# Folding a linear-attention weight by head groups instead of by 128-row blocks

## The chip, the cores and the metric

The kernel runs on one core of one Trainium2 chip. The metric is the device time of one execution in microseconds (us). With one core there is one span and one granted clock of the tensor engine per execution. PE is the tensor engine (PEld its weight loads), DVE the vector engine, ACT the scalar engine, POOL GpSimd, SP the sync engine, whose queue issues most DMA transfers. In the profiles `psT` is PSUM, the memory that PE writes, and `reg` and most other names are SBUF; an *eviction* is a copy from PSUM to SBUF by ACT or DVE.

## The reference

```
xn  = layernorm(x)                              # x: 2048 x 640
# A: linear attention, 32 heads of 20
q, k, v = split(xn @ wqkv)                      # each 32 heads x 2048 x 20
pq, pk  = phi(q), phi(k)                        # phi(t) = (t>0 ? t+1 : exp(t)) + 1e-6
kv  = einsum("bhsd,bhse->bhde", pk, v)          # 20 x 20 for each head
den = einsum("bhqd,bhd->bhq", pq, sum_s pk) + 1e-6
s   = concat_heads((pq @ kv) / den) @ wo        # 2048 x 640
# B: gate
g   = silu(relu(xn @ w1) @ w2)                  # w1: 640 x 1728
out = x + s * g
```

The arrays are bfloat16.

## The kernel before

The kernel never forms v. It builds G = xn' pk (640 x 640, "Gram blocks", line 790), then the key-value product as wv' G with everything outside a head's own 20 x 20 block masked to zero (line 805), and multiplies that by wo. The result is a *folded weight* `wf` (640 x 640), in five blocks of 128 rows. An output tile is then one product, pq (already divided by its denominator) times `wf` (line 891), multiplied by the gate and added to x.

A head has 20 rows, so 128 rows hold 6.4 heads. The masked product is made in six chunks of six heads (120 columns; the last has two heads, 40 columns). A block of 128 rows of `wf` always needs two of these chunks, and what the mask doesn't write has to be zero. That is why there is a memset and why each block sums two products:

```python
VR = 6 * DH      # 120
VC = 6           # chunks
# ... cut ...
    def kv_block(c, b):
        # ... cut: n0, n1, nh, r0, m0 of chunk c; five matmuls into ps[b] ...
        sc.op("DVE", lambda eng: eng.tensor_tensor(
            out=kvp[:, c, n0:n1].rearrange("p (h e) -> p h e", e=DH),
            in0=ps[b][:, 0:n1 - n0].rearrange("p (h e) -> p h e", e=DH),
            in1=mv6[:, m0:m0 + nh].unsqueeze(2).to_broadcast([P, nh, DH]), op=ALU.mult),
            R=[("ps", b), ("mv6", m0), ("kvz",)], W=[("kv", c)])

    def W_block(m, b):
        cs = [c for c in range(VC) if VR * c < P * (m + 1) and min(VR * (c + 1), D) > P * m]
        fns = []
        for a in range(2):
            for ci, c in enumerate(cs):
                fns.append(lambda eng, a=a, c=c, ci=ci: eng.matmul(
                    ps[b + a][:, 0:HN], lhsT=kvp[:, c, P * m:P * (m + 1)], rhs=wo_sb[:, c, HN * a:HN * (a + 1)],
                    start=(ci == 0), stop=(ci == len(cs) - 1)))
        # ... cut: the group, then ACT (even m) or DVE (odd m) copies ps to wf[:, m, :] ...

    sc.op("POOL", lambda eng: eng.memset(kvp, 0.0), W=[("kvz",)], extra=[lastG])
    # ... cut ...
    hooks = {
        (0, 0): [kvs],                                    # key-value chunks, division of pq
        (1, 0): [lambda: W_block(0, 0), lambda: W_block(1, 2)],
        (1, 1): [lambda: W_block(2, 0), lambda: W_block(3, 2)],
        (1, 2): [lambda: W_block(4, 0)],
        (2, 0): [s_of(0, 0, 4)],                          # first output tile
        # ... cut ...
    }
```

`sc` is a small scheduler: `R` and `W` are what an operation reads and writes, and it puts in the semaphore waits. A hook `(p, i)` runs after the i-th group of 13 gate matmuls of tile pair p; the folded weight and the output tiles are thus woven between the gate matmuls, and PE goes through all of it in program order.

Of the kernel before, what the change touches and what calls it, by code (L numbers as in the profile page):

```python
# [5 lines left out]
ACTF = mybir.ActivationFunctionType  # L6
# [14 lines left out]
class Sched:  # L21
# [69 lines left out]

    def _hazards(self, R, W):
        agents = []
        for key in R:
            st = self.res.get(key)
            if st is not None and st.w is not None:
                agents.append(st.w)
        for key in W:
            st = self.res.get(key)
            if st is not None:  # L100
                if st.w is not None:
                    agents.append(st.w)
                agents.extend(st.r.values())
        return agents

    def _update_res(self, agent, R, W):
        Rset = set(R)
        for key in R:
            st = self.res.get(key)
            if st is None:  # L110
                st = self.res[key] = _Res()
            rk = agent if agent[0] == "D" else agent[0]
            st.r[rk] = agent
            st.nread += 1
        for key in W:
            st = self.res.get(key)
            if st is None:
                st = self.res[key] = _Res()
            else:
                assert (st.w is None or st.nread > 0 or key in Rset or key in self.allow_unread  # L120
                        or (agent[0] == "PE" and st.w[0] == "PE")), (
                    "unread overwrite of %r by %r (prev writer %r)" % (key, agent, st.w))
            st.w = agent
            st.r = {}
            st.nread = 0

    def op(self, E, fn, R=(), W=(), extra=()):
        return self.group(E, [fn], R, W, extra)

# [85 lines left out]
def bass_recurrent_scan__linear_attn_block__dense_activation_relu__prompt_kernel(  # L215
# [9 lines left out]
    Bb, S, D = A_x.shape  # L225
# [4 lines left out]
    P = 128  # L230
    T = S // P
    J = S // 512
    C = D // P
# [3 lines left out]
    HN = D // 2  # L237
    EPS_LN = 1e-5
    XR = 8
    VR = 6 * DH  # L240
    VC = 6
# [16 lines left out]
    reg3 = nc.alloc_sbuf_tensor("reg3", [P, T * D], bf)  # L258
    pk = reg3[:, :].rearrange("p (t n) -> p t n", t=T)
    kvp = reg3[:, 0:VC * D].rearrange("p (c n) -> p c n", c=VC)  # L260
# [3 lines left out]
    pqT = nc.alloc_sbuf_tensor("pqT", [P, C, S], bf)  # L264
# [12 lines left out]
    wf = reg6[:, C * D:2 * C * D].rearrange("p (c n) -> p c n", c=C)  # L277
# [4 lines left out]
    wo_sb = reg7[:, 0:VC * D].rearrange("p (c n) -> p c n", c=VC)  # L282
# [17 lines left out]
    mv6 = nc.alloc_sbuf_tensor("mv6", [P, 8], f32)  # L300
# [13 lines left out]
    ps = [psT[:, 512 * i:512 * (i + 1)] for i in range(8)]  # L314

    def ps2(b, n):
        return psT[:, 512 * b:512 * (b + 2)].rearrange("p (a n) -> p a n", a=2)[:, :, 0:n]
# [4 lines left out]
    sc = Sched(nc, NDS)  # L322
    nds = [0]

    def dma(E, fn, R=(), W=(), extra=()):
        i = nds[0]
        nds[0] += 1
        return sc.dma(E, fn, i, R=R, W=W, extra=extra)

    def tok(t):  # L330
        return slice(P * t, P * (t + 1))
# [34 lines left out]
    for k in range(KA, C):  # L366
# [15 lines left out]
          R=[("ident",)], W=[("ident",)])  # L382
# [341 lines left out]
    for j in range(J):  # L724
        for n, item in enumerate(plans[j]):
# [33 lines left out]
            if j == J - 1 and n == 0:  # L759
                for c in range(VC):  # L760
                    r0 = VR * c if c < VC - 1 else D - P
                    dma("SP", lambda eng, c=c, r0=r0: eng.dma_start(wo_sb[:, c, :], A_wo[r0:r0 + P, :]),
                        W=[("wo", c)], extra=[last_norm[0]])
# [12 lines left out]
    for a in range(2):  # L776
# [3 lines left out]
            W=[("w2", a)], extra=[lastW1])  # L780
    for u in range(2):
        dma("ACT", lambda eng, u=u: eng.dma_start(w2l[64 * u:64 * (u + 1), :], B_w2[NF * P:FF, :]),
            W=[("w2l", u)], extra=[lastW1])


    def G_block(k, b):
        fns = []
        for t in range(T):
            for a in range(2):
                fns.append(lambda eng, t=t, a=a: eng.matmul(  # L790
                    ps[b + a][:, 0:HN], lhsT=xn[:, t, P * k:P * (k + 1)], rhs=pk[:, t, HN * a:HN * (a + 1)],
                    start=(t == 0), stop=(t == T - 1)))
        ag = sc.group("PE", fns, R=[("xn", t) for t in range(T)] + [("pk", t) for t in range(T)],
                      W=[("ps", b), ("ps", b + 1)])
        sc.op("DVE", lambda eng: eng.tensor_copy(GT[:, k, :].rearrange("p (a n) -> p a n", a=2), ps2(b, HN)),  # L795
              R=[("ps", b), ("ps", b + 1)], W=[("GT", k)])
        return ag

    def kv_block(c, b):
        n0 = VR * c  # L800
        n1 = min(n0 + VR, D)
        nh = (n1 - n0) // DH
        r0 = VR * c if c < VC - 1 else D - P
        m0 = 0 if c < VC - 1 else 6
        sc.group("PE", [(lambda eng, k=k: eng.matmul(ps[b][:, 0:n1 - n0], lhsT=wv_sb[:, k, r0:r0 + P],  # L805
                                                     rhs=GT[:, k, n0:n1], start=(k == 0), stop=(k == C - 1)))
                        for k in range(C)], R=[("wv",)] + [("GT", k) for k in range(C)], W=[("ps", b)])
        sc.op("DVE", lambda eng: eng.tensor_tensor(
            out=kvp[:, c, n0:n1].rearrange("p (h e) -> p h e", e=DH),
            in0=ps[b][:, 0:n1 - n0].rearrange("p (h e) -> p h e", e=DH),  # L810
            in1=mv6[:, m0:m0 + nh].unsqueeze(2).to_broadcast([P, nh, DH]), op=ALU.mult),
            R=[("ps", b), ("mv6", m0), ("kvz",)], W=[("kv", c)])

    def W_block(m, b):
        cs = [c for c in range(VC) if VR * c < P * (m + 1) and min(VR * (c + 1), D) > P * m]
        fns = []
        for a in range(2):
            for ci, c in enumerate(cs):
                fns.append(lambda eng, a=a, c=c, ci=ci: eng.matmul(  # L819
                    ps[b + a][:, 0:HN], lhsT=kvp[:, c, P * m:P * (m + 1)], rhs=wo_sb[:, c, HN * a:HN * (a + 1)],  # L820
                    start=(ci == 0), stop=(ci == len(cs) - 1)))
        sc.group("PE", fns, R=[("wo", c) for c in cs] + [("kvz",)] + [("kv", c) for c in cs],
                 W=[("ps", b), ("ps", b + 1)])
        if m % 2 == 0:
            sc.op("ACT", lambda eng: eng.activation(out=wf[:, m, :].rearrange("p (a n) -> p a n", a=2), in_=ps2(b, HN),
                                                    func=ACTF.Copy), R=[("ps", b), ("ps", b + 1)], W=[("wf", m)])
        else:
            sc.op("DVE", lambda eng: eng.tensor_copy(wf[:, m, :].rearrange("p (a n) -> p a n", a=2), ps2(b, HN)),
                  R=[("ps", b), ("ps", b + 1)], W=[("wf", m)])



# [56 lines left out]
    def s_mm(t, lo, hi, b):  # L889
        i = t // 4  # L890
        sc.group("PE", [(lambda eng, c=c: eng.matmul(  # L891
            ps[b][:, 0:hi - lo], lhsT=pqT[:, c, tok(t)], rhs=wf[:, c, lo:hi],
            start=(c == 0), stop=(c == C - 1))) for c in range(C)],
            R=[("pqT", i, c) for c in range(C)] + [("wf", c) for c in range(C)], W=[("ps", b)])

    def s_tile(t, b):
        os_ = so[0] % NOUT
        so[0] += 1
        for a in range(2):
            s_mm(t, HN * a, HN * (a + 1), b + a)  # L900
        s_out(t, os_, 0, 0, D, ps2(b, HN), [("ps", b), ("ps", b + 1)], 2)

    def s_last(t):
        for i in range(3):
            lo, hi = LC[i], LC[i + 1]
            s_mm(t, lo, hi, LB[i])
            s_out(t, NOUT, i, lo, hi, ps[LB[i]][:, 0:hi - lo].unsqueeze(1), [("ps", LB[i])], 1)

    lastG = None
    for k in range(C):  # L910
        lastG = G_block(k, (0, 2, 0, 2, 4)[k])
    sc.op("POOL", lambda eng: eng.memset(kvp, 0.0), W=[("kvz",)], extra=[lastG])
    for jx in range(4):
        dma("SP", lambda eng, jx=jx: eng.dma_start(
            xre[:, 4 * jx:4 * jx + 4, :], x2[512 * jx:512 * (jx + 1), :].rearrange("(t p) n -> p t n", p=P)),
            W=[("xre", jx)], extra=[lastG])

    def s_of(p, u, b):
        return lambda: s_tile(pairs[p][u], b)

    def kvs():
        for c in range(VC):
            kv_block(c, (6, 7, 4, 5, 2, 3)[c])
        for i in (0, 1, 2, 3):
            divide(i)

    hooks = {
        (0, 0): [kvs],
        (1, 0): [lambda: W_block(0, 0), lambda: W_block(1, 2)],
        (1, 1): [lambda: W_block(2, 0), lambda: W_block(3, 2)],  # L930
        (1, 2): [lambda: W_block(4, 0)],
        (2, 0): [s_of(0, 0, 4)],
        (2, 1): [s_of(0, 1, 6)],
        (2, 2): [s_of(1, 0, 4)],
# [60 lines left out]
```

## Time and profile before

| | before |
|---|---|
| time, median of four runs | 223.42 us (223.0 to 223.94) |
| span of the profiled execution | 221.3 us |
| PE busy | 215.9 us, 98% |
| granted clock | 1.00 |
| first gate matmul to first output matmul (below: *the stage*) | 20.80 us |

The page's first part (busy time, share of the span, instructions):

```profile
PE 215.9 (98%) x1437; PEld 134.2 (61%) x1447; DVE 119.2 (54%) x221; ACT 82.9 (37%) x136; POOL 46.9 (21%) x69
```

What PE's matmuls waited for (total us, times, longest), the whole answer of the wait view for PE:

```profile
PE psT L388 <- DVE zero L378: 1.1, 1, 1.1
PE psT L571 <- issue: 0.2, 1, 0.2
```

The chain that ended last, in order of time, through the stage (start, length, engine and line, number of instructions). L842 are gate matmuls, L805 the key-value chunks, L819 the folded weight, L860 the gate's last 64 rows, L891 output tiles:

```profile
132.32 1.77 PE psT L842 x13
134.09 1.43 PE psT L805 x30
135.52 5.30 PE psT L842 x39
140.82 0.65 PE psT L860 x8
141.47 1.87 PE psT L842 x13
143.34 1.09 PE psT L819 x8
144.43 1.77 PE psT L842 x13
146.20 1.09 PE psT L819 x8
147.28 1.77 PE psT L842 x13
149.05 0.54 PE psT L819 x4
149.59 3.53 PE psT L842 x26
153.12 1.36 PE psT L891 x10
```

Every piece is PE and each starts where the one before ends. So in this stage time is the number of matmuls times their spacing: 5.30 us for 39 is 136 ns each; such a place in PE's stream is called a *slot* below. The folded weight takes 1.09 + 1.09 + 0.54 = 2.72 us for 20 matmuls, 136 ns each too. Note the 1.87 us after the eight L860 matmuls, where 13 matmuls usually take 1.77: there the weights go from 64 rows back to 128.

Two groups off the chain matter for the argument (the groups view; the last column is idle time of that engine before them, and what ended it):

```profile
L912 POOL MEMSET reg<- 128x3840 bf16 x1 | 3.3, 3298 | 36.2 <-PE psT L790 36.2
L808 DVE TENSOR_TENSOR reg<-psT,mv 128x120 bf16<-128x120 f32 (+1 forms) x6 | 1.1, 259 | 2.6 <-POOL reg L912 2.6
```

The memset takes 3.3 us, and DVE stands idle 2.6 us for it before the first masked eviction. That is a real wait, of an engine that nothing on the chain is waiting for.

### The profile page before, as it was taken

Reading aid. Unit: us, or ns where it says so; the run is one execution under the profiler, and the core shown is the slowest. Engines: PE = TensorE matmul, PEld = TensorE weight load, DVE = VectorE, ACT = ScalarE, POOL = GpSimd, SP = SyncE. Lnnn points to the kernel's source line nnn. Section 1 sums busy time; section 2 is a strip of 40 time slices with the busy share of each in tenths; the row PEclk is TensorE's granted clock in tenths of the full one; section 3 lists DMA queues with packets and bytes.
Section 4 is the critical chain, followed back from the end, with each engine's and each line's share of the span. In section 5 each row is a group of like instructions: output and inputs, shape, how many; then the busy total and the mean of one; then the engine's idle time right before and its main releaser. Section 6 shows DMA issues by size and latency. Waiting matters only on the chain.

```text
span 221.3 us, 3515 instructions
## 1 busy us (share of the span) xinstructions
PE 215.9 (98%) x1437; PEld 134.2 (61%) x1447; DVE 119.2 (54%) x221; ACT 82.9 (37%) x136; POOL 46.9 (21%) x69
## 2 busy tenths in 40 slices
PE   8999999999999999999999999999999999999993
PEld 7655554555545555444477777677767776776672
DVE  3798967789649999773511125920424240422243
ACT  4596575666655766554512000232021102110211
POOL 2268601220042699930000005000000000000000
PEclk9999999999999999999999999999999999999999
DMA  5988597611002152000199889800100100101012
GB/s 179 291 315 157 129 292 80 181 30 30 3 1 59 30 143 67 0 0 3 44 188 365 293 274 379 294 6 3 59 30 33 59 30 33 44 16 62 0 59 61
DMA packets 27904, 23.91 MB, mean 108 GB/s; under 512 B 12272, under 2 KB 27248, under 8 KB 27888
## 3 DMA queue, kind: packets, MB, share of 16 engines
q1 hardware_dynamic: 24656, 19.50, 31.5%
q10 hardware_dynamic: 3232, 4.18, 5.3%
q8 instruction: 11, 0.18, 0.3%
q14 instruction: 5, 0.04, 0.1%
HBM read 15.81 MB, written 5.24 MB: 95 GB/s over the span
## 4 chain that ended last, share of the span: by engine, by line
PE 93%; DMA 2%; SPq 2%; DVE 1%; issue 1%; ACT 0%; ACTq 0%; DVEq 0%
PE psT L842 26%; PE psT L571 25%; PE psT L790 10%; PE psT L549 10%; PE psT L891 9%; PE psT L496 8%; DMA reg<-in_A_x_dram 2%; PE psT L819 1%; PE psT L860 1%; PE psT L588 1%; SPq L359 1%; PE psT L805 1%; SPq L340 1%; PE psT L677 1%; DVE reg L881 0%
## 5 line engine op out<-in xcount | busy, mean ns | idle before, releaser
L842 PE MATMUL psT<-reg,hT 128*128 128x320 bf16 x416 | 60.5, 299 | 0.0
L842 PEld LDWEIGHTS psT<-reg,hT 128*128 128x128 bf16 x416 | 40.3, 98 | 16.5 <-issue 1.1
L571 PE MATMUL psT<-reg 128*128 128x512 bf16 x192 | 45.5, 379 | 0.3 <-issue 0.2
L881 DVE TENSOR_TENSOR reg<-psT,reg 128x640 bf16<-128x640 f32 (+2 forms) x18 | 13.5, 750 | 48.8 <-PE psT L891 47.6
L575 ACT ACTIVATE hT<-psT 128x512 bf16<-128x512 f32 x52 | 30.9, 600 | 18.7 <-PE psT L571 18.7
L571 PEld LDWEIGHTS psT<-reg 128*128 128x128 bf16 x195 | 18.9, 98 | 22.0 <-issue 0.4
L870 ACT ACTIVATE reg<-psT 128x640 bf16<-128x640 f32 x12 | 8.2, 702 | 43.1 <-PE psT L842 23.6
L891 PE MATMUL psT<-reg,pqT 128*128 128x320 bf16 (+2 forms) x165 | 24.4, 295 | 0.0
L507 POOL TENSOR_TENSOR zacc<-zacc,reg 128x640 f32<-128x640 f32 x16 | 23.8, 1488 | 2.3 <-DVE reg L531 1.3
L549 PE MATMUL psT<-reg 128*128 128x512 bf16 x95 | 23.8, 379 | 0.3
L790 PE MATMUL psT<-reg 128*128 128x320 bf16 x160 | 21.9, 299 | 0.0
L891 PEld LDWEIGHTS psT<-reg,pqT 128*128 128x128 bf16 x165 | 16.1, 98 | 5.8
L790 PEld LDWEIGHTS psT<-reg 128*128 128x128 bf16 x160 | 15.7, 98 | 6.2
L513 ACT ACTIVATE regE<-psT 128x640 bf16<-128x640 f32 x24 | 15.6, 701 | 9.1 <-PE psT L496 9.1
L496 PE MATMUL psT<-reg 128*128 128x320 bf16 x120 | 18.3, 299 | 0.0
L557 DVE TENSOR_SCALAR regE<-psT 128x512 bf16<-128x512 f32 x20 | 13.6, 682 | 8.2 <-ACT regE L556 8.2
L559 DVE SCALAR_TENSOR_TENSOR pqT<-regE 128x512 bf16<-128x512 bf16 x20 | 17.4, 869 | 0.7
L870 ACT ACTIVATE reg<-psT,rsy 128x640 bf16<-128x640 f32 x4 | 3.2, 794 | 38.6 <-PE psT L860 33.4
L549 PEld LDWEIGHTS psT<-reg 128*128 128x128 bf16 x100 | 9.8, 98 | 11.5
L496 PEld LDWEIGHTS psT<-reg 128*128 128x128 bf16 x120 | 11.7, 98 | 6.5 <-DMA reg<-reg 0.4
L795 DVE CAST reg<-psT 128x640 bf16<-128x640 f32 x5 | 4.1, 824 | 20.9 <-PE psT L790 20.9
L556 ACT ACTIVATE regE<-psT 128x512 bf16<-128x512 f32 x20 | 12.0, 598 | 8.5 <-PE psT L549 8.5
(68 smaller groups left out, 177.8 us busy)
## 6 DMA issues: line engine op xcount, KB each, us to landing
reg<-in_A_x_dram SPq DMA_DIRECT2D x16, 160.0 KB, 3.1
scr<-regE SPq DMA_DIRECT2D x4, 640.0 KB, 11.1
reg<-in_A_x_dram SPq DMA_DIRECT2D x4, 640.0 KB, 9.3
out_dram<-reg SPq DMA_DIRECT2D x15, 160.0 KB, 1.8
regE<-scr SPq DMA_DIRECT2D x4, 512.0 KB, 5.3
reg<-in_B_w_dram ACTq DMA_DIRECT2D x1, 1120.0 KB, 12.1
reg<-in_B_w_dram ACTq DMA_DIRECT2D x1, 1040.0 KB, 9.1
reg<-in_A_wo_dram SPq DMA_DIRECT2D x6, 160.0 KB, 3.7
```

What stands on the lines that cost most here:

```text
L496: fns.append(lambda eng, a=a, k=k, lhs=lhs: eng.matmul(ps[b + a][:, 0:HN], lhsT=lhs[:, k, tok(t)], rhs=wqk[:, k, D + HN * a:D + HN * (a + 1)],
L507: sc.op("POOL", lambda eng: eng.tensor_tensor(out=zacc[:, :], in0=zacc[:, :], in1=pk[:, t, :], op=ALU.add), R=[("zacc",), ("pk", t)], W=[( ...
L513: sc.op("ACT", lambda eng: eng.activation(out=o_.rearrange("p (a n) -> p a n", a=2), in_=ps2(b, HN), func=func, scale=scale), R=[("ps", b) ...
L549: sc.group("PE", [(lambda eng, k=k: eng.matmul(ps[b], lhsT=wqk[:, k, P * f:P * (f + 1)], rhs=xnT[:, k, schunk(j)], start=(k == 0), stop=(k ...
L557: sc.op("DVE", lambda eng: eng.tensor_scalar(out=r_, in0=ps[b], scalar1=0.0, scalar2=1e-6, op0=ALU.max, op1=ALU.add), R=[("ps", b), ("er_e ...
L559: sc.op("DVE", lambda eng: eng.scalar_tensor_tensor(out=pqT[:, f, schunk(j)], in0=e_, scalar=1.0, in1=r_, op0=ALU.min, op1=ALU.add), R=[(" ...
L571: a = sc.group("PE", [(lambda eng, k=k: eng.matmul(ps[b], lhsT=w1_sb[:, k, P * f:P * (f + 1)], rhs=src[:, k, :], start=(k == 0), stop=(k = ...
L575: sc.op("ACT", lambda eng: eng.activation(out=hT[:, f, schunk(j)], in_=ps[b], func=ACTF.Relu), R=[("ps", b)], W=[("hT", j, f)])
L790: fns.append(lambda eng, t=t, a=a: eng.matmul(ps[b + a][:, 0:HN], lhsT=xn[:, t, P * k:P * (k + 1)], rhs=pk[:, t, HN * a:HN * (a + 1)], sta ...
L842: sc.group("PE", [(lambda eng, f=f: eng.matmul(ps[b][:, 0:HN], lhsT=hT[:, f, tok(t)], rhs=w2_sb[:, f, HN * n:HN * (n + 1)], start=(f == 0 ...
L881: sc.op("DVE", lambda eng: eng.tensor_tensor(out=tmpo[:, os_, lo:hi].rearrange(shp, a=na), in0=src, in1=g_sb[:, t, lo:hi].rearrange(shp, a ...
L891: sc.group("PE", [(lambda eng, c=c: eng.matmul(ps[b][:, 0:hi - lo], lhsT=pqT[:, c, tok(t)], rhs=wf[:, c, lo:hi], start=(c == 0), stop=(c = ...
```

## The change

A chunk's masked product is non-zero only in its own 120 rows and columns. The change makes one pass for each chunk: 120 columns of weights, two matmuls (640 output columns in two halves), no accumulation, 12 matmuls instead of 20. Only columns that the mask has written are read, so the zero fill goes. The price: a pass yields rows 120c to 120c+119 of the folded weight at partitions 0 to 119, while the output matmuls want blocks of 128 rows. Ten SBUF to SBUF transfers move them, cut where a pass crosses a block boundary. The passes are also moved one place earlier.

```diff
--- before.py
+++ after.py
@@ -809,24 +809,32 @@
             out=kvp[:, c, n0:n1].rearrange("p (h e) -> p h e", e=DH),
             in0=ps[b][:, 0:n1 - n0].rearrange("p (h e) -> p h e", e=DH),
             in1=mv6[:, m0:m0 + nh].unsqueeze(2).to_broadcast([P, nh, DH]), op=ALU.mult),
-            R=[("ps", b), ("mv6", m0), ("kvz",)], W=[("kv", c)])
-
-    def W_block(m, b):
-        cs = [c for c in range(VC) if VR * c < P * (m + 1) and min(VR * (c + 1), D) > P * m]
-        fns = []
-        for a in range(2):
-            for ci, c in enumerate(cs):
-                fns.append(lambda eng, a=a, c=c, ci=ci: eng.matmul(
-                    ps[b + a][:, 0:HN], lhsT=kvp[:, c, P * m:P * (m + 1)], rhs=wo_sb[:, c, HN * a:HN * (a + 1)],
-                    start=(ci == 0), stop=(ci == len(cs) - 1)))
-        sc.group("PE", fns, R=[("wo", c) for c in cs] + [("kvz",)] + [("kv", c) for c in cs],
-                 W=[("ps", b), ("ps", b + 1)])
-        if m % 2 == 0:
-            sc.op("ACT", lambda eng: eng.activation(out=wf[:, m, :].rearrange("p (a n) -> p a n", a=2), in_=ps2(b, HN),
-                                                    func=ACTF.Copy), R=[("ps", b), ("ps", b + 1)], W=[("wf", m)])
+            R=[("ps", b), ("mv6", m0)], W=[("kv", c)], extra=[lastG])
+
+    wtmp = reg3[:, VC * D:2 * VC * D].rearrange("p (c n) -> p c n", c=VC)
+    wkeys = []
+
+    def W_block(c, b):
+        n0 = VR * c
+        n = min(VR, D - n0)
+        sc.group("PE", [(lambda eng, a=a: eng.matmul(
+            ps[b + a][0:n, 0:HN], lhsT=kvp[:, c, n0:n0 + n], rhs=wo_sb[:, c, HN * a:HN * (a + 1)],
+            start=True, stop=True)) for a in range(2)], R=[("wo", c), ("kv", c)], W=[("ps", b), ("ps", b + 1)])
+        dst = wtmp[0:n, c, :].rearrange("p (a n) -> p a n", a=2)
+        if c % 2 == 0 or c == 1:
+            sc.op("ACT", lambda eng: eng.activation(out=dst, in_=ps2(b, HN)[0:n], func=ACTF.Copy),
+                  R=[("ps", b), ("ps", b + 1)], W=[("wtmp", c)])
         else:
-            sc.op("DVE", lambda eng: eng.tensor_copy(wf[:, m, :].rearrange("p (a n) -> p a n", a=2), ps2(b, HN)),
-                  R=[("ps", b), ("ps", b + 1)], W=[("wf", m)])
+            sc.op("DVE", lambda eng: eng.tensor_copy(dst, ps2(b, HN)[0:n]), R=[("ps", b), ("ps", b + 1)],
+                  W=[("wtmp", c)])
+        q = n0
+        while q < n0 + n:
+            e = min(n0 + n, (q // P + 1) * P)
+            key = ("wf", q)
+            wkeys.append(key)
+            dma("SP", lambda eng, q=q, e=e: eng.dma_start(wf[q % P:q % P + e - q, q // P, :],
+                                                          wtmp[q - n0:e - n0, c, :]), R=[("wtmp", c)], W=[key])
+            q = e
 
 
 
@@ -891,7 +899,7 @@
         sc.group("PE", [(lambda eng, c=c: eng.matmul(
             ps[b][:, 0:hi - lo], lhsT=pqT[:, c, tok(t)], rhs=wf[:, c, lo:hi],
             start=(c == 0), stop=(c == C - 1))) for c in range(C)],
-            R=[("pqT", i, c) for c in range(C)] + [("wf", c) for c in range(C)], W=[("ps", b)])
+            R=[("pqT", i, c) for c in range(C)] + wkeys, W=[("ps", b)])
 
     def s_tile(t, b):
         os_ = so[0] % NOUT
...
-    sc.op("POOL", lambda eng: eng.memset(kvp, 0.0), W=[("kvz",)], extra=[lastG])
     for jx in range(4):
         dma("SP", lambda eng, jx=jx: eng.dma_start(
             xre[:, 4 * jx:4 * jx + 4, :], x2[512 * jx:512 * (jx + 1), :].rearrange("(t p) n -> p t n", p=P)),
@@ -926,9 +933,9 @@
 
     hooks = {
         (0, 0): [kvs],
-        (1, 0): [lambda: W_block(0, 0), lambda: W_block(1, 2)],
-        (1, 1): [lambda: W_block(2, 0), lambda: W_block(3, 2)],
-        (1, 2): [lambda: W_block(4, 0)],
+        (0, 1): [lambda: W_block(0, 4), lambda: W_block(1, 6)],
+        (1, 0): [lambda: W_block(2, 0), lambda: W_block(3, 2)],
+        (1, 1): [lambda: W_block(4, 0), lambda: W_block(5, 2)],
         (2, 0): [s_of(0, 0, 4)],
         (2, 1): [s_of(0, 1, 6)],
         (2, 2): [s_of(1, 0, 4)],
```

## The prediction

> **What bounds the kernel.** The tensor engine (PE). The page's first part gives PE 215.9 us busy of a 221.3 us span (98%); the chain that ended last is 93% PE; the wait view for PE holds 1.3 us in all; the granted clock is 1.00. From 132 to 153 us, where the change acts, the timeline shows no PE gap. So only PE instruction slots count, and any new PE wait.
>
> **What is removed.** The folded-weight matmuls. Before, five groups of 8, 8 and 4 (20 in all, 128x320): the chain in order of time gives 1.09, 1.09 and 0.54 us, together 2.72 us, 136 ns each. (The Trainium skill, "TensorE: Matmul & The Clock Gate", section "Back-to-back issue gap", gives N/2.4 + 2.5 ns, 136 ns for 320 columns; the trace agrees.) After, six passes of two matmuls, 12 in all, none accumulating: an estimated 12 x 136 = 1.63 us. Saved: 8 x 136 = 1.09 us, all on the chain. Fewer output rows (120, 40) do not make a matmul shorter: the 320 moving columns set it. Changing the weights' shape costs a little: after the 64-row group, 13 gate matmuls take 1.87 us instead of 1.77; the one 40-row pass may cost 0.1 us likewise.
>
> **The memset** (POOL, 3.30 us at 132.4) holds DVE's first masked eviction for 2.6 us, but PE doesn't wait for that: the 39 matmuls after it run at 136 ns. Its removal gives DVE slack, no time.
>
> **What is added.** Six evictions instead of five (ACT 0.70, DVE 0.82 us each, idle engines); the Silu table load (1.28 us) now follows the first two evictions on ACT, ending near 141. Ten SBUF to SBUF transfers on the SP queue, about 0.8 MB. Each occupies the queue about 0.43 us (160 KB loads in the SP timeline).
>
> **The new wait.** The first output matmul now waits for ten transfers. Estimated order: passes 0,1 at 137.3, passes 2,3 at 143.9, passes 4,5 at 146.2 to 146.7; evicted by about 147.7; the last three transfers issued by 149; landing 1.8 us later (160 KB output writes; the Trainium skill, "DMA: Bandwidth & Descriptors", "Anatomy of one DMA", has about 2.0 us fixed for the software-issued path), so near 151. PE has 39 gate matmuls (5.3 us) after the last pass, so it asks at about 152.0. About 1 us of slack: it should just hold. Ten semaphore waits before one matmul should be hidden by PE's queue: the five waits of a query block near 85 us left no gap in the chain.
>
> **Prediction.** 223.67 - 1.09 + 0.1 = 222.7 us (0.4% less). Range 222.0 to 223.7. Chances: faster by over 2% 0.01, within 2% 0.97, slower by over 2% 0.02.
>
> **What would show it.** Right: PE 8 matmuls fewer, folded-weight pieces of the chain about 1.6 us in place of 2.72; the first output matmuls start near 151.9 instead of 152.96, with no DMA in PE's waits; everything later shifts by the same 1 us; SP shows ten transfers landing by about 151. Wrong: PE waiting at the first output matmul for a transfer between its own buffers, or an issue gap there of some tenths.
>
> **What would make it wrong.** SBUF to SBUF transfers landing in 3 us or more, or a queue occupied longer than 0.43 us per issue: each us beyond the slack costs one us of PE. Second, the ten waits costing 0.3 us or more. Third, weights of 120 columns loading so slowly that they aren't hidden under 136 ns matmuls (up to 0.1 us per pass).

## The result, and the profile after

The changed kernel took 222.6 us (median of four runs, 222.55 to 222.66), against 223.42 us. The ratio is 0.9962 with a 95% interval of 0.9938 to 0.9986. All ratios here are the mean time of one kernel's fast runs over that of the other kernel's in the same rounds, so not quite the ratio of the medians.

The page's first part:

```profile
PE 214.9 (97%) x1429; PEld 133.6 (61%) x1439; DVE 119.7 (54%) x221; ACT 83.5 (38%) x137; POOL 43.5 (20%) x68
```

The whole wait view for PE has no transfer in it (L471 and L388 are at the kernel's start):

```profile
PE psT L388 <- DVE zero L378: 1.0, 1, 1.0
PE psT L471 <- DVE reg L462: 0.7, 1, 0.7
PE psT L571 <- issue: 0.2, 1, 0.2
```

The chain in order of time, through the same stage (L850 gate, L805 chunks, L820 folded weight, L868 the gate's last 64 rows, L899 output):

```profile
132.86 1.77 PE psT L850 x13
134.63 1.43 PE psT L805 x30
136.06 1.77 PE psT L850 x13
137.83 0.54 PE psT L820 x4
138.38 3.53 PE psT L850 x26
141.91 0.65 PE psT L868 x8
142.56 1.87 PE psT L850 x13
144.43 0.54 PE psT L820 x4
144.97 1.77 PE psT L850 x13
146.74 0.65 PE psT L820 x4
147.39 5.40 PE psT L850 x39
152.79 1.36 PE psT L899 x10
```

The stage went from 153.12 - 132.32 = 20.80 us to 152.79 - 132.86 = 19.93 us: 0.87 us less. Eight matmuls fewer are worth 8 x 136 ns = 1.09 us. The missing 0.21 us stands in two lines: the last piece of L820 takes 0.65 us where its sisters take 0.54, and the 39 gate matmuls after it take 5.40 us where before they took 5.30. That pass's second half is the one with 40 columns.

The spans differ by only 0.5 us, not 0.87, for two reasons. First, the stage began 0.54 us later in this execution. The chain says why: the first load of x, on which the first layernorm waits, took 4.96 us on the chain here and 4.40 us in the profile before. This differs between executions of one kernel too (the stage begins at 132.70 us here and at 131.81 in the profile of `after_again`), and is why the stage is the better measure below. Second, the tail, from the first output matmul to the end of the span, took 68.16 us here and 68.35 before, 0.19 us less; so 0.54 - 0.87 - 0.19 = -0.52. The difference lies in the last output writes and is no chance of these two profiles: the tail is 68.15 to 68.17 us in every profile with the ten transfers (except `late_two`, which has a slow clock there) and 68.35 to 68.59 in the three without them (`before`, `no_transfers`, `before_twelve`). Its cause was not looked into and stays open.

The lines that answer to the memset and the masked evictions (groups view):

```profile
L808 DVE TENSOR_TENSOR reg<-psT,mv 128x120 bf16<-128x120 f32 (+1 forms) x6 | 1.4, 268 | 1.2 <-PE psT L805 1.2
```

DVE's evictions now wait 1.2 us for their own matmuls and no longer for POOL. The ten transfers on SP's queue (timeline: start, length, the issues merged in one line):

```profile
138.87 11.73 SPq L835 DMA_DIRECT2D reg<-reg  x10
```

The last issue thus ends at 150.60 us. One single issue takes 0.52 to 0.98 us. The DMA view gives the time from issue to landing for some of the ten: 7.5 and 6.1 us for two of the first three, issued while the loads of x still kept the DMA engines busy (mean share 0.98 from 130 to 139 us and 1.06 from 139 to 144), and 1.8 to 2.2 us for those issued later. That the loads are the reason was not tested; the early ones had time to spare. The first output matmul starts at 152.63 us by the timeline.

### The profile page after: what moved, and what is told of

It reads as the page before. It is cut to its first block, busy times and chain, and to the rows that moved or that the text cites. A ratio compares the mean times of both kernels' runs of the same rounds, so it can differ in the third digit from the quotient of the medians.

```text
span 220.8 us, 3513 instructions
## 1 busy us (share of the span) xinstructions
PE 214.9 (97%) x1429; PEld 133.6 (61%) x1439; DVE 119.7 (54%) x221; ACT 83.5 (38%) x137; POOL 43.5 (20%) x68
## 4 chain that ended last, share of the span: by engine, by line
PE 92%; DMA 2%; SPq 2%; DVE 1%; issue 1%; ACT 0%; ACTq 0%; DVEq 0%
PE psT L850 26%; PE psT L571 25%; PE psT L790 10%; PE psT L549 10%; PE psT L899 9%; PE psT L496 8%; DMA reg<-in_A_x_dram 2%; PE psT L868 1%; PE psT L588 1%; SPq L359 1%; PE psT L820 1%; PE psT L805 1%; SPq L340 1%; PE psT L677 1%; DVE reg L889 0%
## 5 line engine op out<-in xcount | busy, mean ns | idle before, releaser
L850 PE MATMUL psT<-reg,hT 128*128 128x320 bf16 x416 | 60.5, 299 | 0.0
L850 PEld LDWEIGHTS psT<-reg,hT 128*128 128x128 bf16 x416 | 40.2, 98 | 16.6 <-issue 1.3
L899 PE MATMUL psT<-reg,pqT 128*128 128x320 bf16 (+2 forms) x165 | 24.4, 295 | 0.0
L899 PEld LDWEIGHTS psT<-reg,pqT 128*128 128x128 bf16 x165 | 16.1, 98 | 5.8
L417 DVE BATCH_NORM_STATS2 stats<-reg 128x6 f32<-128x320 bf16 x32 | 14.0, 474 | 2.0 <-DMA reg<-in_A_x_dram 2.0
```

Of the source, the lines that this page charges most:

```text
L417: sc.op("DVE", lambda eng: eng.bn_stats(stats[:, t, a, :], xv[:, HN * a:HN * (a + 1)]), R=[("xin", t % XR)], W=[("stats", t, a)])
L850: sc.group("PE", [(lambda eng, f=f: eng.matmul(ps[b][:, 0:HN], lhsT=hT[:, f, tok(t)], rhs=w2_sb[:, f, HN * n:HN * (n + 1)], start=(f == 0 ...
L899: sc.group("PE", [(lambda eng, c=c: eng.matmul(ps[b][:, 0:hi - lo], lhsT=pqT[:, c, tok(t)], rhs=wf[:, c, lo:hi], start=(c == 0), stop=(c = ...
```

## The experiments

The stage is measured from the start of the first gate matmul to the start of the first output matmul, in each profile. The kernel before ran in the same rounds. The experiments came in three batches, each on one chip.

| kernel | stage, us | time, us (median) | ratio to before [95%] | result |
|---|---|---|---|---|
| before | 20.80 | 223.42 | | |
| after | 19.93 | 222.60 | 0.9962 [0.9938, 0.9986] | correct |
| memset_back | 19.93 | 221.93 | 0.9957 [0.9931, 0.9984] | correct |
| eight_back | 21.02 | 223.46 | 1.0011 [0.9985, 1.0037] | correct |
| no_transfers | 19.93 | 222.61 | 0.9979 [0.9953, 1.0004] | wrong |
| pad128 | 19.72 | 222.39 | 0.9960 [0.9933, 0.9987] | correct |
| before_twelve | 19.72 | 222.07 | 0.9940 [0.9913, 0.9967] | wrong |
| narrow_two | 20.14 | 222.73 (one run) | | wrong |
| late_one | 20.48 | 223.05 | 0.9981 [0.9947, 1.0015] | correct |
| late_two | 22.56 | 226.34 | 1.0113 [1.0045, 1.0181] | correct |
| late_two_split | 21.92 | 224.28 | 1.0050 [1.0030, 1.0070] | correct |
| after_again | 19.93 | 222.00 | 0.9962 [0.9938, 0.9986] | correct |
| pad128_again | 19.72 | 221.80 | 0.9943 [0.9923, 0.9963] | correct |

The theory: only PE's instruction slots count in this stage, so the gain is the eight matmuls, less 0.2 us for the change of weight shape at the 40-column pass; everything else is hidden behind PE's work. The rivals: the memset's removal helps; the ten transfers, or the ten semaphore waits before the first output matmul, take some of the gain; the 0.2 us is something else.

### The memset back in

```diff
-            R=[("ps", b), ("mv6", m0)], W=[("kv", c)], extra=[lastG])
+            R=[("ps", b), ("mv6", m0), ("kvz",)], W=[("kv", c)], extra=[lastG])
...
+    sc.op("POOL", lambda eng: eng.memset(kvp, 0.0), W=[("kvz",)], extra=[lastG])
```

> The changed kernel with the memset of the key-value matrix back in its old place, and the masked evictions waiting for it. Theory (only PE slots count): same as the changed kernel, ratio to the kernel before about 0.996, 19.9 us from the first gate matmul after the Gram blocks to the first output matmul, as in the changed kernel (20.8 before), although the evictions start 1 us later. Rival (the memset's removal gives part of the gain): this stage grows towards 20.8 us.

The wait is back, by the groups view:

```profile
L808 DVE TENSOR_TENSOR reg<-psT,mv 128x120 bf16<-128x120 f32 (+1 forms) x6 | 1.1, 261 | 2.6 <-POOL reg L920 2.6
```

The stage is 19.93 us, as without it. A 3.3 us memset and a 2.6 us wait of DVE cost nothing here, to 0.01 us.

### Eight matmuls back

```diff
-            start=True, stop=True)) for a in range(2)], ...
+            start=True, stop=True)) for _ in range(2 if c < 4 else 1) for a in range(2)], ...
```

> The changed kernel with passes 0 to 3 issuing their two matmuls twice, so 20 matmuls again, same result. Theory: eight slots of 136 ns return, the stage is 19.93 + 1.09 = 21.0 us, time about 0.1% over the kernel before (ratio 1.000 to 1.002). Rival (the gain comes from something other than the number of matmuls): stays near 0.996.

The stage is 21.02 us, 1.09 more than the changed kernel's; each of the first two pairs of passes takes 1.09 us in the chain instead of 0.54. The time returns to that of the kernel before (1.0011).

### The transfers left out

```diff
-        q = n0
-        while q < n0 + n:
-            ...  # the transfers of this pass, key added for each
+        wkeys.append(("wtmp", c))
```

> Wrong result on purpose: the ten SBUF to SBUF transfers are left out, the output matmuls wait for the six evictions only and read stale weights. Theory (the transfers are hidden behind 39 gate matmuls): the stage stays 19.9 us, ratio 0.996. Rival (ten waits or late transfers cost part of the gain): 0.1 us or more shorter.

The stage is again 19.93 us: the transfers cost PE nothing in the changed kernel. Six waits remain in this run instead of ten; that ten cost nothing is also seen from `pad128` (ten) and `before_twelve` (five), both at 19.72 us. The ratio of the times, 0.9979, is not the 0.996 expected; its interval covers that of the changed kernel, and the tail after the stage took 68.41 us here, 0.25 more than in the changed kernel.

### Every pass 128 columns wide

```diff
+        m0 = n0 if c < VC - 1 else D - P
-            ps[b + a][0:n, 0:HN], lhsT=kvp[:, c, n0:n0 + n], ...
+            ps[b + a][:, 0:HN], lhsT=kvp[:, c, m0:m0 + P], ...
-        dst = wtmp[0:n, c, :]...
+        lo = 0 if c < VC - 1 else 64
+        hi = n if c < VC - 1 else P
+        dst = wtmp[lo:hi, c, :]...
...  # cut: the two evictions read rows lo to hi likewise
-                                   wtmp[q - n0:e - n0, c, :]), ...
+                                   wtmp[q - m0:e - m0, c, :]), ...
```

The surplus columns hold old, finite data; the rows that they give are never moved, so the result is correct.

> Correct result: every pass takes 128 columns as weights, the last one the last 128 columns, and the rows that are not wanted are dropped at the eviction. Theory (the 40-column pass costs two switches of weight shape, 0.11 us into and 0.10 us out of it): its piece of the chain shrinks from 0.65 to 0.54 us, the 39 gate matmuls after it from 5.40 to 5.30 us, the stage from 19.93 to 19.7 us; ratio about 0.995. Rival (the extra 0.2 us is the semaphore waits before that pass, or chance): no change.

The two pieces in question, in its chain (L821 the folded weight, L853 the gate):

```profile
147.26 0.54 PE psT L821 x4
147.81 5.30 PE psT L853 x39
```

Both have lost their excess, and the stage is 19.72 us, 0.21 less. Weight loads of 120 columns themselves cost nothing: this view of the passes' instructions (nanoseconds, least/median/most) shows them slower in the changed kernel than the 97 to 98 ns of 128 columns,

```profile
L820 PEld LDWEIGHTS psT<-reg x12: 95/133/133, 137.5 to 147.0; 128*120 128x120 bf16 x10, 128*40 128x40 bf16 x2
```

yet a group of four such matmuls still takes 0.54 us. The Trainium skill, "TensorE: Matmul & The Clock Gate", section "Weight-path perf modes — Fast Weight Load (FWL) and DoubleRow", says that the fast load is on when the number of weights is 128. The 133 ns for 120 columns against 98 for 128 agree in direction; under a 136 ns matmul the longer load is hidden.

### A second narrow pass

```diff
+        nw = 40 if c == 1 else n
-            ps[b + a][0:n, 0:HN], lhsT=kvp[:, c, n0:n0 + n], ...
+            ps[b + a][0:nw, 0:HN], lhsT=kvp[:, c, n0:n0 + nw], ...
```

> Wrong result on purpose: the changed kernel with pass 1 too taking only 40 columns of weights. Theory (each change of weight shape costs about 0.1 us into it and 0.1 us out of it): the piece of passes 0 and 1 grows from 0.54 to 0.65 us and the 26 gate matmuls after it from 3.53 to 3.63 us; stage 20.14 us. Rival (the 0.2 us belonged to the place of the last pass): stage 19.93 us.

Now the first pair of passes and the gate matmuls after it show the same excess (L821 the passes, L851 the gate):

```profile
137.82 0.65 PE psT L821 x4
138.47 3.64 PE psT L851 x26
```

The stage is 20.14 us, another 0.21. So it is the narrow weights and not the place (this is the profile of a single execution, but pieces of this stage that a change leaves alone repeat to 0.01 us from profile to profile). The Trainium skill, "TensorEngine Tiling (Array Packing)", section "Key Properties", says that changing the tiling mode drains the engine. That would fit if 40 columns are run in another mode than 120 and 128, since only the 40-column matmuls lose time; but no view here shows the mode. The run shows the cost, 0.11 us into and 0.10 us out of the narrow pass; that it is a drain is the page's word and not shown.

### The kernel before, with 12 matmuls

```diff
+        cs = cs if m == 4 else cs[:1]
         fns = []
```

> Wrong result on purpose: the kernel before, its memset, its five evictions straight into the folded weight and all else as they were, but 12 folded-weight matmuls instead of 20 (for the first four blocks one key-value group instead of two). Theory (eight slots are the whole gain): the stage from the first gate matmul to the first output matmul is 20.80 - 1.09 = 19.71 us, as in the padded kernel, ratio about 0.995. Rival (the memset, the evictions or the new order give a part): stage longer than 19.9 us.

The stage is 19.72 us: 20.80 - 1.08. Each of its three pieces of folded weight takes 0.54 us in the chain. With the memset, the direct evictions and the old order all in place, the eight matmuls alone give the whole gain of the stage. It also equals the padded kernel: re-laying the rows by DMA costs PE nothing.

### How near the transfers are to costing something

```diff
-        (1, 1): [lambda: W_block(4, 0), lambda: W_block(5, 2)],
+        (1, 2): [lambda: W_block(4, 0), lambda: W_block(5, 2)],     # late_one
+        (1, 3): [lambda: W_block(4, 4), lambda: W_block(5, 2)],     # late_two
```

> Correct result: the changed kernel with passes 4 and 5 one place (13 gate matmuls, 1.77 us) later. Theory (transfers occupy their queue 0.5 to 0.85 us each in turn and land 1.8 to 2.2 us after the start of their issue, which left under 1 us of slack): the last transfer lands near 153.0 on the changed kernel's time scale, where the output matmul asks at 152.6, so PE waits 0.2 to 0.7 us for a transfer, stage 20.1 to 20.6 us, ratio 0.997 to 1.000. Rival (the slack was 1.8 us or more): stage 19.93 us and no wait.

> Correct result: passes 4 and 5 two places later, directly before the gate matmuls that the first output matmuls follow (other banks, so that no eviction holds PE). Theory: the last transfer is issued near 153.2 and lands near 155.1, PE waits 2.0 to 2.8 us, stage 22 to 22.8 us, ratio 1.005 to 1.010: the gain is gone and more. Rival (transfers land in 1.8 us side by side, not queued): a wait of 1.2 us or less.

One place (1.77 us) later, PE waits. Its wait view, and the end of the chain up to the first output matmul:

```profile
PE psT L899 <- DMA reg<-reg: 0.4, 1, 0.4
```

```profile
147.98 0.71 ACT reg L825
148.69 0.02 issue
148.71 0.55 SPq L835
149.26 0.04 issue
149.30 0.82 SPq L835
150.13 0.04 issue
150.17 2.13 DMA reg<-reg
152.30 0.05 issue
152.35 1.53 PE psT L899 x10
```

This chain is to be read downwards: ACT evicts pass 4, SP issues that pass's two transfers one after the other, then the last transfer, issued at 150.17, lets PE go on at 152.35, which is 2.18 us later. The last issue of the changed kernel ends at 150.60 and takes 0.75 us, so it starts at 149.85; 2.18 us later is 152.03, and PE asked at 152.63. The changed kernel's slack is therefore an estimated 0.6 us. The DMA packets in the traces bear it out: the last one ends 0.37 us before PE goes on in both late kernels, and at 151.65 in the changed kernel, which again gives 152.02. (In the padded kernel, where PE asks 0.21 us earlier, the same estimate leaves 0.4 us.) The loss agrees: a delay of 1.77 us would leave a wait of 1.17, but a later pass 4 no longer stands behind a gate eviction on ACT (0.41 us by the timelines), nor its transfers behind those of pass 3 on SP's queue (0.14 us). That leaves an estimated 0.6, and the stage grew by 0.55 us. The wait view says 0.4 because it counts from the modelled end of the matmul before, which lies 0.16 us after the time at which the next could have started.

Two places later, the stage grew by 2.63 us, as expected, and the time by more: 226.34 us, 1.1% over the kernel before. The chain, from the last transfer on:

```profile
152.89 2.12 DMA reg<-reg
155.01 0.05 issue
155.06 2.27 PE psT L899 x10
157.33 2.70 PE psT L850 x13
160.03 1.36 PE psT L899 x10
```

After the wait of 2.47 us, 10 matmuls took 2.27 us instead of the 1.53 that they took after the short wait of `late_one`, and 13 took 2.70 instead of 1.77. The windows view (us, then busy time of each engine with counts, granted clock, DMA share, GB/s) has the reason in the column before the last two:

```profile
150.00:155.00 5.00, 2.59 (x18) 1.35 (x16) 0.82 (x1) 1.30 (x2) 0.00 (x0) 1.00 0.14 41
156.00:157.00 1.00, 1.00 (x5) 0.60 (x4) 0.00 (x0) 0.00 (x0) 0.00 (x0) 0.50 0.07 16
158.00:159.00 1.00, 1.00 (x6) 0.54 (x5) 0.69 (x2) 0.00 (x0) 0.00 (x0) 0.50 0.00 0
160.00:161.00 1.00, 1.00 (x10) 0.73 (x8) 0.00 (x0) 0.00 (x0) 0.00 (x0) 1.00 0.10 35
```

The granted clock fell to half for about three us, after PE had resumed. From the first output matmul to the end of the span this execution took 69.85 us, where the changed kernel took 68.16. I had expected a ratio of 1.010 at most and measured 1.0113, whose interval covers 1.010; the pause was forecast rightly, the price of the slow clock after it, 1.69 us in this profile, was not forecast at all. It seems not to come every time: the four executions had mean clocks of 0.990, 0.997, 0.990 and 0.992 and took 226.67, 224.37, 226.0 and 227.4 us.

### One of the late transfers from another queue

```diff
-            dma("SP", lambda eng, q=q, e=e: ...
+            dma("ACT" if q == 512 else "SP", lambda eng, q=q, e=e: ...
```

> Correct result: as the kernel with passes 4 and 5 two places late, but one of the last three transfers (88 rows) is issued from ACT's queue, so that the last one leaves SP's queue 0.8 us earlier. Theory (PE resumes 2.2 us after the start of the last issue, and issues go one after another): PE waits about 1.6 to 1.8 us instead of 2.47 us; and if a shorter pause no longer lowers the granted clock, the matmuls after it run at 136 ns and the tail after the first output matmul is 68.2 us instead of 69.85. Rival (the landing, not the issue, is what takes time): the wait stays 2.4 us or more.

PE waited 1.8 us, the stage is 21.92 us, 0.64 less, and the tail after the first output matmul is 68.17 us: the clock stayed at 1.00 (0.999 to 1.000 in the four executions). So the serial issue on one queue was a good part of the wait. The gain is a little less than the 0.8 us of the issue that was moved: that issue took 1.38 us on ACT's queue and, like the last one on SP's queue, ended near 152.4. And a pause of 1.8 us left the clock alone in all four executions, where one of 2.5 us lowered it in three of four, if means of 0.992 and below are read so (0.996 to 0.998 occurs in ordinary executions of several kernels).

### Both good versions once more

> The changed kernel, once more, beside the padded one on the same chip. Theory: stage 19.93 us, ratio 0.996; the times of single executions spread by some tenths of a us because the first loads of x land at different times, before the first matmul of the block.

> The padded kernel once more, same chip. Theory: stage 19.72 us, 0.2 us or 0.1% under the changed kernel, a difference that the spread of the times may hide; ratio 0.995. Rival (padding does nothing): the same stage as the changed kernel.

The stages repeated to the hundredth: 19.93 and 19.72 us. The single times spread (221.55 to 222.87 and 221.18 to 222.37 us), so the 0.2 us between the two is not resolved by the times: the ratios 0.9962 and 0.9943 have overlapping intervals. The stage resolves it in both pairs of profiles. The padded kernel beats both kernels there, by 0.21 us and 1.08 us.

## Why the prediction was right

- **What bounds it.** Right. PE's slots alone set the stage; one experiment added eight matmuls, another took eight away, and they moved it by 1.09 and 1.08 us.
- **What is removed.** Right: 12 matmuls at 136 ns, 0.54 us for each group of four; eight slots are 1.09 us.
- **The memset.** Right: "Its removal gives DVE slack, no time" (memset_back, 19.93 us both ways).
- **The 40-row pass.** Right in kind, mis-sized: "may cost 0.1 us". It cost 0.11 us going in and 0.10 us coming out, 0.21 in all (pad128, narrow_two). I had counted only one switch, because in the profile before only the return from the 64-row group was visible as an excess. So the stage fell by 0.87 us and not by 0.99.
- **The transfers.** Hidden, as forecast (no_transfers), but the margin was mis-sized. I took 0.43 us per issue and 1.8 us to land, so "near 151" and "about 1 us of slack". An issue took 0.52 to 0.98 us, and PE could go on 2.18 us after the start of the last one, at an estimated 152.0: 0.6 us of slack. Two of the first transfers even took 6.1 and 7.5 us to land, but they were early. My scale was too optimistic at both places; it held because the last transfer still landed within the 5.4 us of gate matmuls that follow the last pass.
- **Ten waits.** Right: no cost (`pad128` and `before_twelve`, both 19.72 us).
- **"The first output matmuls start near 151.9."** Wrong in absolute time, 152.63, mainly because this execution's stage began 0.54 us later. Measured from there, 19.93 us against 151.9 - 132.16 = 19.74, it was 0.19 us late; the prediction's own sum, 20.80 - 1.09 + 0.1 = 19.81, was 0.12 us short, which is the second switch.
- **The time.** 222.7 us forecast, 222.6 measured. So close a hit is partly luck. The forecast started from 223.67 us, one execution of the kernel before, whose median is 223.42; the stage gave 0.12 us less than forecast and the tail 0.19 us that nobody forecast; and the starts of single executions vary by some tenths of a us, as much as these errors.

Still open: why the first loads of x land at different times; why the tail is shorter with the ten transfers; and whether the clock falls by the length of a pause alone or also by when it comes. None of these was tried by itself.

## What to carry to other kernels

Where one engine is busy without gaps, count its instruction slots: accumulating two half-empty products cost two full slots here, and re-laying rows by DMA was free because enough work of that engine lay between the last eviction and the first use. Work out that distance with the issue time per transfer included, because issues on one queue ran one after another (0.52 to 0.98 us each here, where 0.43 had been assumed), and look at what else keeps the DMA engines busy then. Avoid a narrow weight among full ones, padding with unused columns if need be: 40 columns cost 0.21 us a pass here, 120 cost nothing. And don't let PE pause for microseconds: in the profile with a pause of 2.5 us the slow clock after it cost another 1.7.

## What the Trainium skill lacked or had wrong

- "TensorE: Matmul & The Clock Gate", section "Why this matters for your kernels", warns of idle gaps over about 3 us. Here one of 2.47 us, shorter than that, was followed by about three us at half clock and 1.69 us lost (the profile of late_two; by their mean clock, three of its four executions); one of 1.8 us was not (late_two_split).
- "TensorEngine Tiling (Array Packing)", section "Key Properties", says that a change of tiling mode drains the engine but gives no cost. Here going from 120 columns of weights to 40 and on to 128 cost 0.11 + 0.10 us, if that is such a change.
- "DMA: Bandwidth & Descriptors", section "Anatomy of one DMA — SWDGE (gpsimd) path", gives about 2.0 us of fixed cost for the software path only; for the hardware queue the page has a first-byte latency but no time to completion. From the hardware queue, an SBUF to SBUF transfer of 40 rows of 1280 B let its reader go on 2.18 us after the start of its issue.
- No page that I found gives the time that an issue occupies SP's queue. Output writes of 128 rows took 0.33 to 0.42 us. The SBUF to SBUF transfers of 16, 32 and 96 rows took 0.52 to 0.59 us, those of 8, 24, 40, 88, 104 and 120 rows 0.72 to 0.99 us (112 rows: 0.56 to 0.84 us); rows in multiples of 16 look cheaper, but this was not tried by itself.
